# Clustered attention with a gated FFN behind it: transfers reordered over two queues, loads three pairs deep, RMS work in single steps

## The chip, the core and the metric

The kernel runs on one core of a Trainium2 chip. The core has five engines, each with its own in-order queue: TensorE (PE, its weight loads shown as PEld), VectorE (DVE), ScalarE (ACT), GpSimd (POOL) and SyncE (SP). SP does no arithmetic here, it issues DMA transfers; ACT and POOL issue some as well. The metric is the device time of one execution in microseconds, lower is better.

## What is computed

```python
# q, k, v: (4, 8, 768, 64) f32; centroids: (8, 16, 64) f32
q_assign = argmax(einsum('bhsd,hcd->bhsc', q_n, c_n), -1)   # q_n, k_n, c_n: rows scaled to norm 1
k_assign = argmax(einsum('bhsd,hcd->bhsc', k_n, c_n), -1)
mask = q_assign[:, :, :, None] == k_assign[:, :, None, :]
scores = where(mask, q @ k.T / 8, -1e9)
attn_out = softmax(scores) @ v                              # (4, 8, 768, 64)
x = attn_out.transpose(0, 2, 1, 3).reshape(3072, 512)
xn = x / sqrt(mean(x * x, -1) + 1e-6) * rms_g
g = xn @ w_gate                                             # 512 x 1536
out = (g * sigmoid(g) * (xn @ w_val)) @ w_out               # 1536 x 512, out (3072, 512) f32
```

Queries attend only to keys whose nearest of 16 centroids is the same one.

## The kernel before

The 32 slots (4 batches of 8 heads) run in order, two heads making a pair, 16 pairs in all. The scores of a slot are 768 x 768, cut into 9 chunks of 512 columns. One chunk is one step of the main loop, so a slot has 9 steps, a pair 18, a batch 72, all of it 288 steps. A schedule written out by hand sets the order on every engine: `at(step, fn)` hangs a piece of work on a step, and each engine does its instructions in the order in which the program emits them.

A step holds: the chunk's score matmuls (`score_chunk`, L241) and the exp of them on ACT (L244), one piece of the FFN if one is due (`ffn_next`), one group of the PV matmuls of the slot before (`pv_group`, L255, in steps 2 to 7 of a slot), at step 8 of a slot the division by the row sums on DVE (`pv_norm`, L264 and L265), and then what hangs on the step.

What hangs on steps, by pair: `load_pair` brings q, k and v of a pair from HBM (five transfers, 3 x 384 KB). The eight parts of `prep_parts` prepare a pair two pairs ahead of its use: three groups of four transposes on TensorE (`t_group`, L172, with a copy out of PSUM on DVE or ACT, L175 and L177), the bf16 casts on POOL (L182), the routing matmuls against the centroids (`assign`, sp, L195), two parts of argmax on DVE that end in ohT (L202 to L215), and the cast of v (L186). The second argmax part issues eight small transfers that put the one-hot rows under the operands (`aug<-ohT`, L220). These added rows make the score matmul itself subtract the mask. The parts of pair `pi` hang on steps 0, 2, 4, 5, 8, 9, 11 and 9 behind `18 * (pi - 2)`; pairs 0 and 1 are prepared ahead of the loop.

By batch: `rms_parts` has six sums of squares (ACT and DVE by turns, L279 and L282), the inverse root on POOL (`ir`, L287 and L288), then the scaled rows xn on DVE (L296), each followed by a transposing transfer into xnT, issued by SP (L298). These follow a batch's last pair, at steps 9 to 15 of the next batch. The FFN of a batch begins `LAG` steps into the next batch, one piece a step: a gate group gp, a value group vp (L318, four matmuls each), and, for the half batch before, an output group dp (L347). tanh of gp is on ACT (L323), the products uu and gvT on DVE (L327 and L333). The FFN of the last batch runs alone behind the loop. The FFN's first half batch reads three of the six xn transposes.

Weights come in twelve transfers from POOL's queue (`w_load`), which also turn them into bf16: four each of wg, wv and wo. PSUM holds two transpose buffers (`ps_t`, shared by t_group and assign), two for scores, two for gp and vp, one each for the PV sums and dp.

Of the kernel before, what the change touches and what calls it, by code (L numbers as in the profile page):

```python
# [9 lines left out]
BF16 = mybir.dt.bfloat16  # L10
AX = mybir.AxisListType.X
ALU = mybir.AluOpType
# [7 lines left out]
def kernel(  # L20
# [12 lines left out]
    nc = tc.nc  # L33
    B, H, S, D = q.shape
    NC = centroids.shape[1]
    DM, DF = moe_w_gate.shape
    P = 128
# [11 lines left out]
    out_v = out.rearrange("(b p t) d -> b p t d", b=B, t=ST)  # L49

    const = ctx.enter_context(tc.tile_pool(name="const", bufs=1))
    ld = ctx.enter_context(tc.tile_pool(name="ld", bufs=2))
    prep = ctx.enter_context(tc.tile_pool(name="prep", bufs=2))
    small = ctx.enter_context(tc.tile_pool(name="small", bufs=2))
    ptp = ctx.enter_context(tc.tile_pool(name="ptp", bufs=2))
# [10 lines left out]

    loads = {}

    def load_pair(pi, eng2=None):
        b, hp = divmod(pi, NP)  # L70
        tiles = []
        for src, nm, eng in ((q, "q_in", nc.sync), (k, "k_in", eng2 or nc.sync)):
            tl = ld.tile([P, ST, 2, D], F32, name=nm, tag=nm)
            for a in range(2):
                eng.dma_start(out=tl[:, :, a, :],
                              in_=src[b, 2 * hp + a].rearrange("(p t) d -> p t d", p=P))
            tiles.append(tl)
        tl = ld.tile([P, 2, ST * D], F32, name="v_in", tag="v_in")
        nc.sync.dma_start(
            out=tl, in_=v[b, 2 * hp:2 * hp + 2].rearrange("h (p t) d -> p h (t d)", p=P))  # L80
        tiles.append(tl)
        loads[pi] = tiles

    c_in = const.tile([P, D], F32, name="c_in")
    nc.scalar.dma_start(out=c_in, in_=centroids.rearrange("h c d -> (h c) d"))
    load_pair(0, nc.scalar)
    load_pair(1)
    g_b = const.tile([P, DM], F32, name="g_b")


# [68 lines left out]
    def prep_parts(pi):  # L159
        st = pi % NSET  # L160
        qk32 = [None]
        parts = []

        def t_group(g):
            if g == 0:
                qk32[0] = prep.tile([P, 2 * S], F32, name="qk32", tag="qk32")
            q_in, k_in, v_in = loads[pi]
            tp = ps_t.tile([P, 4, P], F32, name="tp", tag="t")
            for i in range(4):
                side, t = divmod(4 * g + i, ST)  # L170
                src = (q_in, k_in)[side]
                nc.tensor.transpose(tp[:, i, :], src[:, t, :, :].rearrange("p a d -> p (a d)"), ident_f)  # L172
            dst = qk32[0][:, g * 512:(g + 1) * 512]
            if g == 1 or pi < 5:
                nc.vector.tensor_copy(dst, tp[:, :, :].rearrange("p a b -> p (a b)"))  # L175
# [12 lines left out]

        state = {}

        def assign():
            hp = pi % NP
            sp = ps_t.tile([P, HS], F32, name="sp", tag="t")
            for j in range(4):
                nc.tensor.matmul(sp[32 * j:32 * j + 32, :], lhsT=cbd[:, hp, :],  # L195
                                 rhs=qk32[0][:, j * HS:(j + 1) * HS], start=True, stop=True,
                                 tile_position=(0, 32 * j))
            state["sp"] = sp

        def argmax1():  # L200
            tr = prep.tile([P, HS], F32, name="tr", tag="tr")
            nc.vector.transpose(tr, state["sp"])  # L202
            mx = small.tile([P, HS // NC], F32, name="mx", tag="mx")
            trv = tr[:, :].rearrange("p (n c) -> p n c", c=NC)
            nc.vector.tensor_reduce(mx, trv, axis=AX, op=ALU.max)
            state["tr"], state["mx"] = trv, mx

        def argmax2():
            oh = prep.tile([P, HS], BF16, name="oh", tag="oh")
# [5 lines left out]
            nc.vector.transpose(ohT, oh)  # L215
            for a in range(2):
                for j in range(4):
                    side, half = divmod(j, 2)
                    eng = nc.scalar if pi == 0 and a else nc.sync
                    eng.dma_start(  # L220
                        out=aug[st][a][O0[a]:O0[a] + NC, side, half * HS:(half + 1) * HS],
                        in_=ohT[32 * j + NC * a:32 * j + NC * a + NC, :])
# [48 lines left out]
    def rms_parts(b):  # L271
        st = {}

        def sumsq(t):
            if t == 0:
                st["ss"] = small.tile([P, ST], F32, name="ss", tag="ss")
                st["jk"] = xp.tile([P, 2, DM], BF16, name="jk", tag="jk")
            if t % 2 == 0:
                nc.scalar.activation(st["jk"][:, 0, :], x_t[b][:, t, :], ACT.Square,  # L279
                                     accum_out=st["ss"][:, t:t + 1])  # L280
            else:
                nc.vector.scalar_tensor_tensor(st["jk"][:, 1, :], x_t[b][:, t, :], 1.0, x_t[b][:, t, :],  # L282
                                               op0=ALU.mult, op1=ALU.mult, accum_out=st["ss"][:, t:t + 1])

        def inv():
            ir = small.tile([P, ST], F32, name="ir", tag="ir")
            nc.gpsimd.tensor_scalar(ir, st["ss"], scalar1=1.0 / DM, scalar2=eps, op0=ALU.mult, op1=ALU.add)  # L287
            nc.gpsimd.tensor_tensor(ir, ir, mhalf, op=ALU.pow)  # L288
            st["ir"] = ir

        def norm(m):
            if m == 0:
                xnT[b] = xp.tile([P, DC, S], BF16, name="xnT", tag="xnT")
            for t in range(m * TH, (m + 1) * TH):
                xn = xp.tile([P, DM], BF16, name="xn", tag="xn", bufs=ST)
                nc.vector.scalar_tensor_tensor(xn, x_t[b][:, t, :], st["ir"][:, t:t + 1], g_b,  # L296
                                               op0=ALU.mult, op1=ALU.mult)
                nc.sync.dma_start_transpose(xnT[b][:, :, t * P:(t + 1) * P], xn)  # L298

        return [lambda t=t: sumsq(t) for t in range(ST)] + [inv, lambda: norm(0), lambda: norm(1)]  # L300


    gvT = {}
# [75 lines left out]
    def at(step, fn):  # L379
        extra.setdefault(step, []).append(fn)  # L380

    for i, part in enumerate(prep_parts(0)):
        part()
        if i == 1:
            put_centroids()
    for i, part in enumerate(prep_parts(1)):
        part()
    for a in range(2):
        nc.vector.memset(aug[2][a], 0.0)
    load_pair(2)  # L390
    load_pair(3)
    nc.sync.dma_start(out=g_b, in_=moe_rms_g.unsqueeze(0).to_broadcast([P, DM]))
    for pi in range(2, B * NP):
        base = 2 * NCH * (pi - 2)
        for fn, step in zip(prep_parts(pi), (0, 2, 4, 5, 8, 9, 11, 9)):
            at(base + step, fn)
        if pi + 2 < B * NP:
            at(base + 12, lambda pi=pi: load_pair(pi + 2))
    for i in range(12):
        at(3 + 6 * i, lambda i=i: w_load(i))  # L400
    for b in range(B):
        steps = (9, 9, 10, 10, 11, 11, 12, 13, 15)
# [59 lines left out]
```

## Time and profile before

| what | value |
|---|---|
| three runs | 401.71, 405.21 and 406.61 us; median 405.21 |
| the profiled execution | 406.12 us, its span 404.3 us |
| TensorE busy | 347.4 us (86% of the span) |
| ScalarE, VectorE, GpSimd busy | 229.8, 224.7 and 76.3 us |
| mean granted TensorE clock | 0.958 of full speed |
| DMA | 35.40 MB, mean 88 GB/s |

Rows of the profile are read so. A timeline row has start, length, engine, line, operation, output <- input, count, and in brackets how long the engine stood idle before and what released it. "SPq" is SP issuing a transfer, not the transfer itself. A row of the chain of waits has start, length and what it was. A row of busy time by stretch gives the stretch, its length, the busy time and the number of instructions of each engine, the granted clock of TensorE, the mean busy share of the 16 DMA engines and the GB/s. A row of a line's instructions gives the shortest, median and longest in ns. Rows of a DMA queue give packets, MB and the time of its packets as a share of 16 engines over the stretch.

### The profile page before, as it was taken

Reading aid. Unit: us, or ns where it says so; the run is one execution under the profiler, and the core shown is the slowest. Engines: PE = TensorE matmul, PEld = TensorE weight load, DVE = VectorE, ACT = ScalarE, POOL = GpSimd, SP = SyncE. Lnnn points to the kernel's source line nnn. Section 1 sums busy time; section 2 is a strip of 40 time slices with the busy share of each in tenths; the row PEclk is TensorE's granted clock in tenths of the full one; section 3 lists DMA queues with packets and bytes.
Section 4 is the critical chain, followed back from the end, with each engine's and each line's share of the span. In section 5 each row is a group of like instructions: output and inputs, shape, how many; then the busy total and the mean of one; then the engine's idle time right before and its main releaser. Section 6 shows DMA issues by size and latency. Waiting matters only on the chain.

```text
span 404.3 us, 7577 instructions
## 1 busy us (share of the span) xinstructions
PE 347.4 (86%) x2880; PEld 209.6 (52%) x2913; DVE 224.7 (56%) x443; ACT 229.8 (57%) x441; POOL 76.3 (19%) x80
## 2 busy tenths in 40 slices
PE   2706996884699999979999999989999996999996
PEld 1304664553456656546565656555666653555542
DVE  5542664347155665694647564876545577655540
ACT  1004997696367877666676767756777741222231
POOL 1531455531202030312021212303000001000000
PEclk9955999899689999999999999999999999999999
DMA  9129799973804042319150605041100004110011
GB/s 192 54 53 244 140 214 191 201 127 97 184 12 123 16 116 53 101 38 182 47 147 7 170 14 147 6 96 42 35 29 28 2 26 92 40 53 26 26 54 78
DMA packets 78212, 35.40 MB, mean 88 GB/s; under 512 B 66272, under 2 KB 73952, under 8 KB 78176
## 3 DMA queue, kind: packets, MB, share of 16 engines
q1 hardware_dynamic: 73584, 29.72, 29.8%
q0 software_dynamic: 2752, 4.72, 6.9%
q10 hardware_dynamic: 1840, 0.48, 0.6%
q8 instruction: 23, 0.38, 0.4%
q14 instruction: 13, 0.11, 0.1%
HBM read 28.61 MB, written 6.29 MB: 86 GB/s over the span
## 4 chain that ended last, share of the span: by engine, by line
PE 70%; DVE 9%; ACT 6%; DMA 6%; SPq 4%; issue 3%; POOL 1%; POOLq 0%; ACTq 0%; DVEq 0%
PE gp L318 14%; PE vp L318 14%; PE dp L347 13%; PE sc L241 13%; PE acc L255 7%; PE tp L172 5%; ACT pT L244 5%; PE sp L195 4%; DMA k_in<-in_k_dram 4%; DVE xn L296 3%; SPq L220 2%; DMA xnT<-xn 1%; DVE uu L327 1%; DVE jk L282 1%; DVE gvT L333 1%
## 5 line engine op out<-in xcount | busy, mean ns | idle before, releaser
L244 ACT ACTIVATE pT<-sc 128x512 bf16<-128x512 f32 x288 | 165.4, 597 | 96.4 <-PE sc L241 94.9
L241 PE MATMUL sc<-aug 128*128 128x512 bf16 (+1 forms) x384 | 111.3, 336 | 5.6 <-ACT pT L244 4.7
L327 DVE SCALAR_TENSOR_TENSOR uu<-th,gp 128x384 f32<-128x384 f32 x96 | 53.1, 553 | 81.7 <-ACT th L323 81.7
L318 PE MATMUL vp<-xnT,wv 128*128 128x384 bf16 x384 | 78.7, 328 | 6.6 <-DVE gvT L333 6.3
L318 PE MATMUL gp<-xnT,wg 128*128 128x384 bf16 x384 | 78.7, 328 | 5.9 <-DMA xnT<-xn 4.2
L255 PEld LDWEIGHTS <-pT 128*128 128x128 bf16 x1152 | 63.2, 100 | 38.2 <-DVE x L265 4.6
L182 POOL CAST aug<-qk 64x1536 bf16<-64x1536 f32 x32 | 46.8, 1464 | 178.1 <-ACT qk L177 98.5
L323 ACT ACTIVATE th<-gp 128x384 f32<-128x384 f32 x96 | 47.2, 492 | 56.5 <-PE gp L318 53.9
L347 PE MATMUL dp<-wo,gvT 128*128 128x512 bf16 x255 | 71.0, 379 | 4.9 <-DVE ob L355 2.2
L255 PE MATMUL acc<-vbf,pT 128*128 128x65 bf16 x1152 | 69.4, 196 | 4.2 <-DVE x L265 4.0
L333 DVE TENSOR_TENSOR gvT<-uu,vp 128x384 bf16<-128x384 f32 x96 | 52.7, 549 | 7.0 <-PE vp L318 1.6
L318 PEld LDWEIGHTS <-wg 128*128 128x128 bf16 x384 | 37.3, 98 | 35.7 <-issue 7.8
L318 PEld LDWEIGHTS <-wv 128*128 128x128 bf16 x384 | 37.4, 98 | 27.3 <-issue 9.0
L241 PEld LDWEIGHTS <-aug 128*128 128x128 bf16 x384 | 34.6, 100 | 20.5 <-issue 6.3
L347 PEld LDWEIGHTS <-gvT 128*128 128x128 bf16 x288 | 27.9, 97 | 29.5 <-issue 4.6
L175 DVE COPY qk<-tp 128x512 f32<-128x512 f32 x26 | 17.9, 690 | 39.4 <-PE tp L172 39.4
L172 PE MATMUL tp<-ident_f,q_in 128*128 128x128 f32 x96 | 18.2, 308 | 18.5 <-DMA q_in<-in_q_dram 18.5
L172 PE MATMUL tp<-ident_f,k_in 128*128 128x128 f32 x96 | 18.9, 313 | 7.3 <-DMA k_in<-in_k_dram 4.7
L172 PEld LDWEIGHTS tp<-ident_f,q_in 128*128 128x128 f32 x96 | 12.7, 157 | 22.9 <-issue 15.9
L296 DVE SCALAR_TENSOR_TENSOR xn<-x,ir,g_b 128x512 bf16<-128x512 bf16 x24 | 16.5, 746 | 4.2 <-POOL ir L288 4.2
L265 DVE TENSOR_TENSOR x<-acc,inv 128x384 bf16<-128x384 f32 x32 | 17.8, 557 | 1.1
L177 ACT COPY qk<-tp 128x512 f32<-128x512 f32 x22 | 12.9, 586 | 7.9 <-PE tp L172 7.9
(48 smaller groups left out, 155.8 us busy)
## 6 DMA issues: line engine op xcount, KB each, us to landing
q_in<-in_q_dram SPq DMA_DIRECT2D x32, 192.0 KB, 3.7
v_in<-in_v_dram SPq DMA_DIRECT2D x16, 384.0 KB, 4.6
out_dram<-ob SPq DMA_DIRECT2D x24, 256.0 KB, 2.0
k_in<-in_k_dram SPq DMA_DIRECT2D x30, 192.0 KB, 4.0
aug<-ohT SPq DMA_DIRECT2D x124, 12.0 KB, 1.8
wg<-in_moe_w_gate_dram POOLq DMA_DIRECT2D x4, 384.0 KB, 5.6
wv<-in_moe_w_val_dram POOLq DMA_DIRECT2D x4, 384.0 KB, 7.7
wo<-in_moe_w_out_dram POOLq DMA_DIRECT2D x4, 384.0 KB, 8.8
```

What stands on the lines that cost most here:

```text
L172: nc.tensor.transpose(tp[:, i, :], src[:, t, :, :].rearrange("p a d -> p (a d)"), ident_f)
L175: nc.vector.tensor_copy(dst, tp[:, :, :].rearrange("p a b -> p (a b)"))
L182: nc.gpsimd.tensor_copy(aug[st][a][r, :, :].rearrange("p s n -> p (s n)"), qk32[0][r, :])
L241: nc.tensor.matmul(sc[:, o:o + n], lhsT=ag[:, 1, kc * P:(kc + 1) * P], rhs=ag[:, 0, qo:qo + n], start=True, stop=True)
L244: nc.scalar.activation(pts[slot][:, j * CH:(j + 1) * CH], sc, ACT.Exp, scale=scale)
L255: nc.tensor.matmul(acc[:, g, :], lhsT=pts[slot][:, kc * S + g * P:kc * S + (g + 1) * P], rhs=vb[:, a, kc, :], start=(kc == 0), stop=(kc == ...
L296: nc.vector.scalar_tensor_tensor(xn, x_t[b][:, t, :], st["ir"][:, t:t + 1], g_b, op0=ALU.mult, op1=ALU.mult)
L318: nc.tensor.matmul(pt[:, :HS], lhsT=w[:, dc, fc * P:(fc + 1) * P], rhs=xnT[b][:, dc, m * HS:(m + 1) * HS], start=(dc == 0), stop=(dc == DC ...
L323: nc.scalar.activation(th, pt[:, :HS], ACT.Tanh, scale=0.5)
L327: nc.vector.scalar_tensor_tensor(uu, th, 1.0, pt[:, :HS], op0=ALU.add, op1=ALU.mult)
L333: nc.vector.tensor_tensor(gvT[half][:, fc, :], uu, pt[:, :HS], op=ALU.mult)
L347: nc.tensor.matmul(dp, lhsT=gvT[hf][:, f, tl * P:(tl + 1) * P], rhs=wo[:, f, :], start=(f == 0), stop=(f == FC - 1))
```

## The change

- The load pool has three buffers of each tensor instead of two.
- The first two pairs' loads: before, SP issued nine and ACT the two of pair 0's k. Now SP issues the two of pair 0's q, and ACT all others.
- Pair 2's load and g_b (the RMS gains) are issued ahead of pair 1's preparation, pair 3's at step 3, pair 4's at step 17, and pair `pi + 2` of the others at step 6 of pair `pi`'s 18 instead of 12.
- Pair 2's own preparation stands six steps later, at steps 6 to 17.
- Weight loads: eight at steps 4, 14, ... 74 and four at 84, 96, 108 and 120, instead of twelve at steps 3, 9, ... 69.
- The copies out of the transpose buffers: pair 0's second one goes to ACT, pair 5's first and third to DVE.
- RMS: one part per step. `norm` does one of six xn and its transposing transfer instead of three; the 13 parts stand at steps 9 to 25 of a batch instead of 9 parts at 9 to 15. xn has three buffers instead of six.
- `LAG` is 26 instead of 24.

```diff
-    ld = ctx.enter_context(tc.tile_pool(name="ld", bufs=2))
+    ld = ctx.enter_context(tc.tile_pool(name="ld", bufs=3))
...
-    load_pair(0, nc.scalar)
-    load_pair(1)
+    load_pair(0, (nc.sync, nc.scalar, nc.scalar))
+    load_pair(1, (nc.scalar, nc.scalar, nc.scalar))
...
-            if g == 1 or pi < 5:
+            if (g == 1) != (pi == 0) or 0 < pi < 6:
                 nc.vector.tensor_copy(dst, tp[:, :, :].rearrange("p a b -> p (a b)"))
...
-        def norm(m):
-            if m == 0:
+        def norm(t):
+            if t == 0:
                 xnT[b] = xp.tile([P, DC, S], BF16, name="xnT", tag="xnT")
-            for t in range(m * TH, (m + 1) * TH):
-                xn = xp.tile([P, DM], BF16, name="xn", tag="xn", bufs=ST)
...
+            xn = xp.tile([P, DM], BF16, name="xn", tag="xn", bufs=3)
...
+    load_pair(2)
+    nc.sync.dma_start(out=g_b, in_=moe_rms_g.unsqueeze(0).to_broadcast([P, DM]))
     for i, part in enumerate(prep_parts(1)):
         part()
...
-    load_pair(2)
-    load_pair(3)
-    nc.sync.dma_start(out=g_b, in_=moe_rms_g.unsqueeze(0).to_broadcast([P, DM]))
...
+        steps = (0, 2, 4, 5, 8, 9, 11, 9) if pi > 2 else (6, 8, 10, 11, 14, 15, 17, 15)
...
-            at(base + 12, lambda pi=pi: load_pair(pi + 2))
+            at(base + 6 if pi > 2 else 17, lambda pi=pi: load_pair(pi + 2))
+    at(3, lambda: load_pair(3))
...
-    LAG = 24
+    LAG = 26
```

How the instructions stand on the engines, before and now. First SP's queue at the program's start, as it was before; the number behind q_in and its like is the buffer of one pair's load, that behind ohT belongs to one pair's routing:

```order
L75 DMA q_in_95<-in_q_dram 128x6x64 x2
L79 DMA v_in_101<-in_v_dram 128x2x384
L75 DMA q_in_103<-in_q_dram 128x6x64 x2
L75 DMA k_in_106<-in_k_dram 128x6x64 x2
L79 DMA v_in_109<-in_v_dram 128x2x384
L220 DMA aug00_125<-ohT_196 16x384 x4
L220 DMA aug10_131<-ohT_240 16x384 x4
L220 DMA aug11_133<-ohT_240 16x384 x4
L75 DMA q_in_253<-in_q_dram 128x6x64 x2
```

The last row is pair 2's load; it stood behind the rows of pair 0 (ohT_196) and pair 1 (ohT_240). The same place of SP's queue now, on to pair 3's load:

```order
L76 DMA q_in_95<-in_q_dram 128x6x64 x2
L221 DMA aug00_125<-ohT_196 16x384 x4
L76 DMA q_in_207<-in_q_dram 128x6x64 x2
L76 DMA k_in_210<-in_k_dram 128x6x64 x2
L80 DMA v_in_213<-in_v_dram 128x2x384
L388 DMA g_b_111<-in_moe_rms_g_dram 128x512
L221 DMA aug10_131<-ohT_249 16x384 x4
L221 DMA aug11_133<-ohT_249 16x384 x4
L76 DMA q_in_276<-in_q_dram 128x6x64 x2
```

Pair 2's load (q_in_207 and the next two) and g_b stand between pair 0's rows and pair 1's, and pair 3's load (q_in_276) behind pair 1's rows. Next SP's queue around the first batch's transposes of xn, before:

```order
L220 DMA aug00_125<-ohT_1148 16x384 x4
L220 DMA aug01_127<-ohT_1148 16x384 x4
L75 DMA q_in_1169<-in_q_dram 128x6x64 x2
L75 DMA k_in_1172<-in_k_dram 128x6x64 x2
L79 DMA v_in_1175<-in_v_dram 128x2x384
L298 DMA_TRANSPOSE xnT_1190<-xn_1191 128x4x128
L298 DMA_TRANSPOSE xnT_1190<-xn_1194 128x4x128
L298 DMA_TRANSPOSE xnT_1190<-xn_1197 128x4x128
```

These are pair 6's rows, pair 8's load and the first three transposes. The same place now:

```order
L76 DMA q_in_1091<-in_q_dram 128x6x64 x2
L76 DMA k_in_1094<-in_k_dram 128x6x64 x2
L80 DMA v_in_1097<-in_v_dram 128x2x384
L221 DMA aug00_125<-ohT_1150 16x384 x4
L221 DMA aug01_127<-ohT_1150 16x384 x4
L298 DMA_TRANSPOSE xnT_1222<-xn_1223 128x4x128
L298 DMA_TRANSPOSE xnT_1222<-xn_1237 128x4x128
L298 DMA_TRANSPOSE xnT_1222<-xn_1244 128x4x128
```

Pair 8's load went from between the rows and the transposes to ahead of the rows. Last DVE's queue at the same place in the program, before (jk are the squares, xn the scaled rows, inv and x the two instructions of `pv_norm`):

```order
L282 SCALAR_TENSOR_TENSOR jk,ss<-x 128x512 x2
L210 TENSOR_TENSOR oh<-tr,mx 128x384
L212 TENSOR_SCALAR oh<-oh 64x384
L215 STREAM_TRANSPOSE ohT<-oh 128x384
L282 SCALAR_TENSOR_TENSOR jk,ss<-x 128x512
L296 SCALAR_TENSOR_TENSOR xn<-x,ir,g_b 128x512 x6
L264 RECIPROCAL inv<-acc 128x6
L265 TENSOR_TENSOR x<-acc,inv 128x6x64
L175 COPY qk_1248<-tp 128x512
```

And now:

```order
L283 SCALAR_TENSOR_TENSOR jk,ss<-x 128x512
L211 TENSOR_TENSOR oh<-tr,mx 128x384
L213 TENSOR_SCALAR oh<-oh 64x384
L216 STREAM_TRANSPOSE ohT<-oh 128x384
L283 SCALAR_TENSOR_TENSOR jk,ss<-x 128x512 x2
L265 RECIPROCAL inv<-acc 128x6
L266 TENSOR_TENSOR x<-acc,inv 128x6x64
L296 SCALAR_TENSOR_TENSOR xn<-x,ir,g_b 128x512 x3
L176 COPY qk_1230<-tp 128x512
L296 SCALAR_TENSOR_TENSOR xn<-x,ir,g_b 128x512 x3
L265 RECIPROCAL inv<-acc 128x6
```

One square went behind ohT, the six xn behind `pv_norm`, and pair 7's copy between the third and the fourth.

More of the change, by code (lines that the diff above doesn't have):

```diff
@@ L67, with load_pair @@
     loads = {}
-    def load_pair(pi, eng2=None):
+    def load_pair(pi, engs=None):
         b, hp = divmod(pi, NP)
+        engs = engs or (nc.sync, nc.sync, nc.sync)
         tiles = []
-        for src, nm, eng in ((q, "q_in", nc.sync), (k, "k_in", eng2 or nc.sync)):
+        for src, nm, eng in ((q, "q_in", engs[0]), (k, "k_in", engs[1])):
             tl = ld.tile([P, ST, 2, D], F32, name=nm, tag=nm)
@@ L78, in load_pair @@
         tl = ld.tile([P, 2, ST * D], F32, name="v_in", tag="v_in")
-        nc.sync.dma_start(
+        engs[2].dma_start(
             out=tl, in_=v[b, 2 * hp:2 * hp + 2].rearrange("h (p t) d -> p h (t d)", p=P))
@@ L289, in inv @@
             st["ir"] = ir
-        def norm(m):
-            if m == 0:
+        def norm(t):
+            if t == 0:
                 xnT[b] = xp.tile([P, DC, S], BF16, name="xnT", tag="xnT")
-            for t in range(m * TH, (m + 1) * TH):
-                xn = xp.tile([P, DM], BF16, name="xn", tag="xn", bufs=ST)
[L296 to L300, printed above, removed]
+            xn = xp.tile([P, DM], BF16, name="xn", tag="xn", bufs=3)
+            nc.vector.scalar_tensor_tensor(xn, x_t[b][:, t, :], st["ir"][:, t:t + 1], g_b,
+                                           op0=ALU.mult, op1=ALU.mult)
+            nc.sync.dma_start_transpose(xnT[b][:, :, t * P:(t + 1) * P], xn)
+        return ([lambda t=t: sumsq(t) for t in range(ST)] + [inv]
+                + [lambda t=t: norm(t) for t in range(ST)])
     gvT = {}
@@ L389 @@
         nc.vector.memset(aug[2][a], 0.0)
-    load_pair(2)
-    load_pair(3)
-    nc.sync.dma_start(out=g_b, in_=moe_rms_g.unsqueeze(0).to_broadcast([P, DM]))
     for pi in range(2, B * NP):
         base = 2 * NCH * (pi - 2)
-        for fn, step in zip(prep_parts(pi), (0, 2, 4, 5, 8, 9, 11, 9)):
+        steps = (0, 2, 4, 5, 8, 9, 11, 9) if pi > 2 else (6, 8, 10, 11, 14, 15, 17, 15)
+        for fn, step in zip(prep_parts(pi), steps):
             at(base + step, fn)
         if pi + 2 < B * NP:
-            at(base + 12, lambda pi=pi: load_pair(pi + 2))
-    for i in range(12):
-        at(3 + 6 * i, lambda i=i: w_load(i))
+            at(base + 6 if pi > 2 else 17, lambda pi=pi: load_pair(pi + 2))
+    at(3, lambda: load_pair(3))
+    for i in range(8):
+        at(4 + 10 * i, lambda i=i: w_load(i))
+    for i in range(4):
+        at(84 + 12 * i, lambda i=i: w_load(8 + i))
     for b in range(B):
-        steps = (9, 9, 10, 10, 11, 11, 12, 13, 15)
+        steps = (9, 10, 11, 12, 13, 14, 15, 17, 18, 19, 21, 23, 25)
         for fn, step in zip(rms_parts(b), steps):
             at(H * NCH * (b + 1) + step, fn)
-    LAG = 24
+    LAG = 26
     def extras(step):
```

## The prediction

> **What bounds the kernel now.** I first asked in which stretches TensorE does nothing, with the table of busy time by stretch.
>
> ```profile
> core 0: us, PE busy (x) PEld busy (x) DVE busy (x) ACT busy (x) POOL busy (x), PEclk, DMA share, GB/s
> 24.00:33.00 9.00, 0.00 (x0) 0.00 (x0) 1.10 (x2) 0.00 (x0) 0.00 (x0) 0.50 0.63 126
> 39.60:50.20 10.60, 9.89 (x121) 6.58 (x121) 6.05 (x11) 9.75 (x19) 5.09 (x7) 1.00 0.79 153
> 60.80:76.70 15.90, 11.46 (x121) 7.47 (x121) 5.31 (x11) 10.85 (x21) 7.10 (x8) 0.89 0.92 179
> 87.80:112.50 24.70, 14.88 (x129) 9.25 (x130) 11.61 (x24) 13.05 (x28) 7.16 (x8) 0.83 0.59 132
> 148.10:168.50 20.40, 20.21 (x184) 12.54 (x187) 11.50 (x25) 14.19 (x27) 4.36 (x5) 1.00 0.30 76
> 168.50:192.80 24.30, 20.74 (x184) 12.51 (x186) 17.63 (x38) 15.53 (x33) 5.72 (x6) 1.00 0.46 92
> 253.90:277.40 23.50, 20.62 (x183) 12.54 (x190) 17.66 (x37) 15.54 (x32) 5.31 (x6) 1.00 0.25 61
> 328.00:341.00 13.00, 9.13 (x58) 4.79 (x58) 11.15 (x23) 3.90 (x10) 1.52 (x2) 1.00 0.20 50
> ```
>
> Rows two to seven are each one pair (18 steps). A pair of attention alone takes 10.6 us, with ACT at 9.75. A pair with all of the FFN beside it takes 20.4, and there TensorE is full: nothing but its work counts. What exceeds these prices is waiting. TensorE's own timeline names it:
>
> ```profile
> 33.16 1.08 PE L172 MATMUL tp<-ident_f,q_in 128*128 128x128 f32 x4 [12.35 <-DMA q_in<-in_q_dram]
> 72.00 0.41 PE L172 MATMUL tp<-ident_f,k_in 128*128 128x128 f32 x2 [3.81 <-DMA k_in<-in_k_dram]
> 100.47 0.51 PE L255 MATMUL acc<-vbf,pT 128*128 128x65 bf16 x6 [4.02 <-DVE x L265]
> 108.30 1.44 PE L318 MATMUL gp<-xnT,wg 128*128 128x384 bf16 x4 [3.52 <-DMA xnT<-xn]
> ```
>
> Who made these late stands in SP's timeline. SP issues one transfer after another: loads, the mask rows (aug<-ohT) and the transposes of xn.
>
> ```profile
> 16.72 11.83 SPq L220 DMA_DIRECT2D aug<-ohT  x12
> 28.65 1.29 SPq L75 DMA_DIRECT2D q_in<-in_q_dram  x2
> 31.42 0.93 SPq L79 DMA_DIRECT2D v_in<-in_v_dram  x1
> 60.93 1.44 SPq L75 DMA_DIRECT2D q_in<-in_q_dram  x2
> 65.51 9.24 SPq L220 DMA_DIRECT2D aug<-ohT  x8
> 74.86 1.30 SPq L75 DMA_DIRECT2D q_in<-in_q_dram  x2
> 93.17 5.98 SPq L220 DMA_DIRECT2D aug<-ohT  x8
> 99.25 1.29 SPq L75 DMA_DIRECT2D q_in<-in_q_dram  x2
> 103.01 7.86 SPq L298 DMA_TRANSPOSE xnT<-xn  x6
> ```
>
> Pair 2's load stands behind both pairs' mask rows until 28.65. The third batch of rows (9.24 us for eight, where six is usual) went into full rings. The first transposes stand behind a load from 99.25 to 103.0. The chain of waits gives the milestones (sp x8 is the routing of a pair, step 8 of its 18):
>
> ```profile
> 17.99 2.30 PE sp L195 x8
> 23.01 0.59 DVE ohT L215
> 40.77 4.28 ACT pT L244 x8
> 87.81 0.78 PE sp L195 x8
> 91.74 0.61 ACT jk L279 x2
> ```
>
> **The start, part by part.** ACT's queue now issues nine loads before ACT's table load, and the second copy of pair 0 moves from DVE to ACT. SP issued nearly the same series before:
>
> ```profile
> 4.15 4.19 SPq L75 DMA_DIRECT2D k_in<-in_k_dram  x2
> 8.39 0.82 SPq L79 DMA_DIRECT2D v_in<-in_v_dram  x1
> 2.56 1.28 ACT L100 ACT_TABLE_LOAD   x1 [2.56 <-issue]
> 9.23 0.69 DVE L175 COPY qk<-tp 128x512 f32<-128x512 f32 x1 [1.27 <-PE tp L172]
> 1.87 6.53 DMA k_in<-in_k_dram
> ```
>
> Pair 1's k was held for 4.19 us, and the last issue ended at 9.2. If ACT is held alike, the table load ends at 10.5 and the copy at about 11.3, against 9.9. TensorE's next transposes need that PSUM buffer, so everything is 1.4 us later, a little of it won back: I take +1.2. The bound on the other side: ACT isn't held, and k, behind no other load on its ring, lands up to 2 us before 8.40: -1.5. The Trainium skill (DMA: Bandwidth & Descriptors, "Issuing engines are not separate DMA queues") says that issuing from several engines saves issue time alone, since all share 16 engines; by that the -1.5 falls away and the sum stays.
>
> Step 0 was at 20.3 (end of pair 1's sp) and is then at 21.5. Pair 2's transposes stand at step 6 instead of 0, so six scores come first, at ACT's 4.28 / 8 = 0.535 us: step 6 at 24.7. On SP, pair 0's four mask rows run from 17.9 at 0.62 each (the last eight of the twelve before ran from ohT's end, 23.60, to 28.55) to 20.4; pair 2's load follows. A load lands in:
>
> ```profile
> q_in<-in_q_dram SPq DMA_DIRECT2D x32, 192.0 KB, 3.7
> ```
>
> Its second q half is issued at 21.1 and lands at 24.8. The 12.35 us wait is gone, to within some tenths.
>
> What is late next: pair 3's load. It needs no buffer any more (three deep), but on SP it stands behind pair 2's load (28.65 to 32.35, 3.8 with the gap: ends 24.2), g_b (one more issue, 0.6) and pair 1's eight rows. These, now queued behind the load, wait until 24.8 for their ohT anyway (23.6 + 1.2) and end at 29.8: issued from 29.9, second q half 30.6, landed 34.3. Step 18 is at 21.5 + 18 x 0.56 = 31.6 (0.56 between 0.535 and 10.6 / 18 = 0.59). TensorE waits 2.7 us; between 0 (steps slower) and 6 (a weight load beside it).
>
> **Attention, steps 18 to 98.** Weights go from one in 6 steps to one in 10. The DMA queues of 45 to 73 us:
>
> ```profile
> q0 software_dynamic: 1470, 3.11, 61.3%
> q1 hardware_dynamic: 7437, 2.60, 39.3%
> ```
>
> q0 is the weights: 17.2 us of the 28 for 3.11 MB, 2.2 per 384 KB. q1 takes 4.2 us per MB, 5.0 for a pair's 1.18 MB (3 x 384 KB). Before, a pair of 10.6 us asked for 3 x 2.2 + 5.0 = 11.6, more than there is; now 1.8 x 2.2 + 5.0 = 9.0, 85%. So I let the 3.81 us wait go and the pace be 10.6 a pair. SP has about 3.8 + 8 x 0.62 = 8.8 us of issue per pair: also fits, and loads 4 to 8 come 4 us or more ahead by that count. Moving pair 5's copies to DVE is hidden (DVE 6 of 10.6). Pair 6's routing (step 80) is at 31.6 + 2.7 + 62 x 0.59 = 70.9, and with pair 6's copies on ACT at 71.3 (the pair from 76.7 to 87.8, which had them, took 11.1), against 87.81.
>
> From there it goes by SP. Its rows began 5.4 us behind sp and were out at 99.15, 11.3 behind it: 82.6 now. The load that followed has moved ahead. For the transposes:
>
> ```profile
> L298 SPq DMA_TRANSPOSE xnT<-xn x24: 1192/1217/2221, 103.0 to 342.6; - x24
> DMA to landing us min/median/max: 2.4/2.5/4.3
> ```
>
> The FFN's first half needs three: the third is issued at 82.6 + 2 x 1.3 = 85.2 and lands at 87.7. TensorE would be at step 98 at 71.3 + 11.1 + 3 x 0.61 (ACT's squares) = 84.2, and waits 3.6 us: **first FFN matmul at 87.8, against 108.3: 20.5 us**. The 4.02 us wait falls away inside this: it was for pv_norm, queued on DVE behind six xn in a row,
>
> ```profile
> 95.66 4.06 DVE L296 SCALAR_TENSOR_TENSOR xn<-x,ir,g_b 128x512 bf16<-128x512 bf16 x6 [1.96 <-POOL ir L288]
> ```
>
> which now come behind that pv_norm. The FFN starts two steps later in the program, so two more scores and PV groups are behind it already: at most 2 x 9.89 / 18 = 1.1 us of TensorE, of which transposes and routing have a part; I take 0.8: 21.3. xn has three buffers, so DVE's fourth waits for the first transpose to land; behind the sixth, which waits for the third transpose (87.7), stands the next pv_norm, 1.5 us on, before PV needs it at step 101.
>
> Clock: TensorE ran at about half after such waits.
>
> ```profile
> 108.00:115.00 7.00, 6.70 (x38) 3.08 (x39) 2.70 (x6) 2.27 (x4) 0.83 (x1) 0.56 0.28 56
> ```
>
> Since I leave a wait of 3.6 us at the same place, I let this stretch stand; without it some 7 x (1 - 0.56) = 3 us more are won. The Trainium skill (TensorE: Matmul & The Clock Gate, "Why this matters for your kernels") puts the limit at gaps of about 3 us: by it the sum has a step there: a second wait of 2.9 instead of 3.6 would give 377.5 - 0.7 - 3.0 = 373.8. The trace agrees as far as it goes (slow after 3.52); no gap of it near 3 us shows the limit.
>
> **RMS behind the FFN.** Three boundaries cost 24.3 - 20.4 = 3.9, 23.5 - 20.4 = 3.1 and 13.0 - 9.13 = 3.9: 10.9. There DVE does its three xn in a row while FFN results wait. One per step fits a 20.4 us pair (DVE 17.6), but DVE is in order and still stands for ir: I leave 1 us at the first two and 2.5 at the last, whose steps are short. Won: 6.4, between 0 and 10.9. The later wo loads (last at step 120, first use at 136) have 16 steps: nothing.
>
> **The sum.** 21.3 + 6.4 = 27.7; span 404.3 - 27.7 = 376.6. The profiled execution took 406.12 and its span is 1.8 less; the median of the runs is 405.21. 378.4 x 405.21 / 406.12 = **377.5**.
>
> **Rivals.** *Full cover*: ACT isn't held (2.7), half of the two waits (3.2) and half of the RMS rest (2.2) go as well, with some clock (1.5): 368. For it: the two waits are small differences between times counted from single rows, and vanish if SP is 0.1 us faster per issue. Against: SP's order makes them. Chance 0.20. *RMS in parts wins nothing*: DVE, waiting for ir or for a transpose with only three buffers, holds up the FFN at each boundary, and a row batch of 9 us doubles the wait at step 98: 377.5 + 6.4 + 3.6 = 387. DVE's share speaks against. 0.15. *The rings stay full*: the loads don't come early because SP is held in issuing, as from 60.93 to 74.86: 13.9 a pair, 4.5 for a load and 9.3 for eight rows. Six loads and five batches from 29.9: 103.4, the FFN at 108.5, and only the 7.2 of the other terms are won: 398. Against: 85% instead of 109% demand. 0.07. *Slower*: the clock in the FFN stage. That stage is 289 us of full TensorE. The row
>
> ```profile
> 109.00:130.00 21.00, 20.46 (x186) 12.70 (x184) 11.16 (x23) 14.32 (x28) 2.46 (x3) 0.88 0.30 73
> ```
>
> shows 0.88 over 21 us of it. Should the denser work be granted 0.88 throughout, 289 / 0.88 adds 39 us: 417. It eats the whole gain below 0.91. Against: 1.00 from 148.1 to 168.5 with TensorE 99% busy. 0.03. The forecast has 0.55.
>
> **Numbers.** A measurement of this kernel tells about 2% from no change, that is 397 to 413. The range takes the forecast with its bounds, most of full cover and the RMS rival: 365 to 392. Faster by over 2%: 0.55 + 0.20 + 0.15 and a little of the third rival, 0.91; same 0.06; slower 0.03.
>
> **What would show it.** No wait of over 1 us for pair 2's q; one of 1 to 5 us for pair 3's q near 32; DMA share under 0.95 from 45 to 73 and pairs of 10.6; first gp at 85 to 91, behind xnT; pairs over an RMS boundary at 21 to 22 us. The forecast is wrong if ACT's first copy comes after 13 us, if eight rows still take 9 us on SP more than once, or if first gp comes after 95.

## The result, and the profile after

The changed kernel takes 386.32 us (median of 4 runs, 384.61 to 389.47) against 405.91 of before (4 runs, 401.71 to 406.98): 19.6 us less; the ratio on record is 0.955, 95% interval 0.947 to 0.963. In the later runs the executions of the kernel before fall into two groups, 399 to 404 us and a slower state of 405 to 412 that their ratios leave out; three of the four here and the profiled one (406.12) lie in the range of the second, so the gains against them are probably some us too large, and fast against fast the changed kernel, run again, is at 0.964 (0.957 to 0.972). The forecast was 377.5 with 365 to 392 around it: the time lies inside, 9 us on the slow side of the forecast. The profiled execution of the changed kernel took 389.47 us, span 387.7, so by the two profiles the gain is 16.6 us against the 27.7 of the sum.

TensorE's timeline of the changed kernel, its long waits of the first 110 us (in brackets the idle time before, and its releaser):

```profile
33.87 0.63 PE L173 MATMUL tp<-ident_f,q_in 128*128 128x128 f32 x4 [1.55 <-DMA q_in<-in_q_dram]
39.06 0.66 PE L173 MATMUL tp<-ident_f,k_in 128*128 128x128 f32 x2 [3.69 <-DMA k_in<-in_k_dram]
102.32 1.44 PE L319 MATMUL gp<-xnT,wg 128*128 128x384 bf16 x4 [12.88 <-DMA xnT<-xn]
```

The waits of 12.35 us (pair 2's q), 3.81 (pair 5's k) and 4.02 (pv_norm behind six xn) are gone. In their place stand 5.2 us for pair 3's load, and one of 12.9 us where the FFN starts: it was 3.5. The first FFN matmul comes at 102.3 instead of 108.3; that is later than the 95 us which the prediction gave as a sign that it is wrong. The chain of waits gives the routing of pairs 2, 3, 4, 5 and 6, and what the FFN waited for:

```profile
29.66 0.78 PE sp L196 x8
44.38 0.78 PE sp L196 x8
55.00 0.78 PE sp L196 x8
65.62 0.78 PE sp L196 x8
76.71 0.78 PE sp L196 x8
...
93.57 1.35 SPq L298
...
95.03 1.28 SPq L298
...
96.40 5.83 DMA xnT<-xn
```

Attention runs at 10.6 us a pair from 44.4 on, as counted. But pair 6's rows, whose routing was at 76.7, were on SP only from 87.7. SP's timeline of the changed kernel:

```profile
40.64 1.29 SPq L76 DMA_DIRECT2D q_in<-in_q_dram  x2
...
44.47 1.23 SPq L76 DMA_DIRECT2D q_in<-in_q_dram  x2
45.79 2.13 SPq L76 DMA_DIRECT2D k_in<-in_k_dram  x2
48.01 3.05 SPq L80 DMA_DIRECT2D v_in<-in_v_dram  x1
51.16 6.45 SPq L221 DMA_DIRECT2D aug<-ohT  x8
57.70 1.30 SPq L76 DMA_DIRECT2D q_in<-in_q_dram  x2
59.10 3.61 SPq L76 DMA_DIRECT2D k_in<-in_k_dram  x2
62.80 2.56 SPq L80 DMA_DIRECT2D v_in<-in_v_dram  x1
65.50 5.71 SPq L221 DMA_DIRECT2D aug<-ohT  x8
...
83.01 1.30 SPq L76 DMA_DIRECT2D q_in<-in_q_dram  x2
...
87.72 5.75 SPq L221 DMA_DIRECT2D aug<-ohT  x8
93.57 4.38 SPq L298 DMA_TRANSPOSE xnT<-xn  x3
```

From 40.6 to the transposes SP has no pause. A load that issues in 3.8 us when free takes 6.6 (from 44.47) and 7.7 (from 57.70). Four pairs, from 44.47 to 93.47, take SP 12.2 us each, where TensorE and ACT need 10.6. SP, which does no arithmetic, sets the pace of the stage.

Behind the start of the FFN it is the other way round; the table by stretch, of the changed kernel (a plain pair, one over the first RMS boundary, the last boundary):

```profile
140.10:160.50 20.40, 20.40 (x186) 12.71 (x184) 11.85 (x24) 14.38 (x28) 3.76 (x3) 1.00 0.30 76
160.50:181.20 20.70, 20.70 (x186) 12.81 (x185) 17.83 (x37) 15.83 (x33) 5.63 (x5) 1.00 0.38 85
304.00:330.00 26.00, 22.23 (x150) 12.11 (x149) 19.55 (x39) 7.45 (x17) 1.52 (x2) 1.00 0.21 51
```

Over the boundary TensorE has no idle time left. At the last one it still stands for 26.0 - 22.2 = 3.8 us.

### The profile page after: what moved, and what is told of

Read it like the earlier page. It is cut to its first block, busy times and chain, and to the rows that moved or that the text cites. A ratio compares the mean times of both kernels' runs of the same rounds, so it can differ in the third digit from the quotient of the medians.

```text
span 387.7 us, 7630 instructions
## 1 busy us (share of the span) xinstructions
PE 344.9 (89%) x2913; PEld 208.2 (54%) x2913; DVE 227.6 (59%) x444; ACT 229.0 (59%) x440; POOL 76.2 (20%) x80
## 4 chain that ended last, share of the span: by engine, by line
PE 80%; ACT 7%; DMA 6%; DVE 3%; SPq 2%; issue 1%; POOLq 0%; POOL 0%; ACTq 0%; DVEq 0%
PE sc L242 16%; PE gp L319 16%; PE dp L348 15%; PE vp L319 15%; PE acc L256 8%; PE tp L173 6%; ACT pT L245 6%; PE sp L196 4%; DMA xnT<-xn 3%; DMA k_in<-in_k_dram 2%; SPq L221 1%; DMA q_in<-in_q_dram 1%; SPq L298 1%; DVE xn L296 1%; ACT jk L280 0%
## 5 line engine op out<-in xcount | busy, mean ns | idle before, releaser
L319 PE MATMUL gp<-xnT,wg 128*128 128x384 bf16 x384 | 78.9, 328 | 15.0 <-DMA xnT<-xn 12.9
L319 PE MATMUL vp<-xnT,wv 128*128 128x384 bf16 x384 | 78.7, 328 | 1.2 <-DVE gvT L334 1.2
L348 PE MATMUL dp<-wo,gvT 128*128 128x512 bf16 x288 | 76.0, 379 | 1.6 <-ACT ob L354 1.1
L256 PE MATMUL acc<-vbf,pT 128*128 128x65 bf16 x1152 | 68.6, 195 | 0.0
L319 PEld LDWEIGHTS <-wg 128*128 128x128 bf16 x384 | 37.5, 98 | 45.6 <-issue 17.4
L319 PEld LDWEIGHTS <-wv 128*128 128x128 bf16 x384 | 37.5, 98 | 26.9 <-issue 2.5
L242 PEld LDWEIGHTS <-aug 128*128 128x128 bf16 x384 | 34.7, 99 | 22.5 <-issue 10.6
L296 DVE SCALAR_TENSOR_TENSOR xn<-x,ir,g_b 128x512 bf16<-128x512 bf16 x24 | 18.9, 812 | 17.2 <-DMA xnT<-xn 16.3
L196 PE MATMUL sp<-qk,cbd 128*32 128x384 f32 x128 | 16.5, 564 | 0.8 <-DVE qk L176 0.8
```

Of the source, the lines that this page charges most:

```text
L242: nc.tensor.matmul(sc[:, o:o + n], lhsT=ag[:, 1, kc * P:(kc + 1) * P], rhs=ag[:, 0, qo:qo + n], start=True, stop=True)
L256: nc.tensor.matmul(acc[:, g, :], lhsT=pts[slot][:, kc * S + g * P:kc * S + (g + 1) * P], rhs=vb[:, a, kc, :], start=(kc == 0), stop=(kc == ...
L319: nc.tensor.matmul(pt[:, :HS], lhsT=w[:, dc, fc * P:(fc + 1) * P], rhs=xnT[b][:, dc, m * HS:(m + 1) * HS], start=(dc == 0), stop=(dc == DC ...
L348: nc.tensor.matmul(dp, lhsT=gvT[hf][:, f, tl * P:(tl + 1) * P], rhs=wo[:, f, :], start=(f == 0), stop=(f == FC - 1))
```

## The experiments

The ideas to be told apart: that weight packets hold SP up (W), that SP simply has too many transfers (S), that the earliest late load costs the time (pair 3's), and how much the change's own parts are worth. "First gp" is the first FFN matmul in each run's own profile. The kernel before, run beside the others on each chip, had medians of 402.6 to 408.4 us.

### No weights on the way

```diff
-            nc.gpsimd.dma_start(out=(wg, wv)[kind][:, j, :], ...)
+            nc.vector.memset((wg, wv)[kind][:, j, :], 0.01)
...
-            nc.gpsimd.dma_start(out=wo[:, 3 * j:3 * j + 3, :], ...)
+            nc.vector.memset(wo[:, 3 * j:3 * j + 3, :], 0.01)
```

> The weights are not loaded: where a weight load stood, DVE fills that part of the weight tile with a constant, so the FFN computes with constants in place of the real weights, at the same size and count of matmuls. Theory W (weight packets fill the rings and hold SP in issuing the loads): a pair's load is issued in 3.3 to 4 us everywhere (6.6, 7.7 and 6.5 us in the changed kernel for pairs 5, 6 and 7), pair 6's mask rows start as soon as their ohT is ready, the third xn transpose lands in 2.5 us instead of 5.8, the first FFN matmul comes at 86 to 91 us instead of 102.3, and the time is 371 to 376 us. Theory S (SP has too many transfers to issue in this stage, whatever else travels): loads still take 6 to 8 us to issue, only the landing gets shorter, first FFN matmul at 98 to 99, time 382 to 384 us.

Measured: 374.08 us (373.46 to 374.72), ratio 0.934 [0.931, 0.938]. SP's and TensorE's timelines of this run (L218, L295 and L316 are the L221, L298 and L319 of the others):

```profile
53.19 1.30 SPq L76 DMA_DIRECT2D q_in<-in_q_dram  x2
54.58 1.91 SPq L76 DMA_DIRECT2D k_in<-in_k_dram  x2
56.59 0.58 SPq L80 DMA_DIRECT2D v_in<-in_v_dram  x1
57.31 5.33 SPq L218 DMA_DIRECT2D aug<-ohT  x8
...
76.06 5.38 SPq L218 DMA_DIRECT2D aug<-ohT  x8
81.53 7.10 SPq L295 DMA_TRANSPOSE xnT<-xn  x5
```

```profile
86.73 0.82 PE L316 MATMUL gp<-xnT,wg 128*128 128x384 bf16 x4 [2.57 <-DMA xnT<-xn]
```

Pair 6's load, 7.7 us to issue with weights beside it, takes 4.0 (53.19 to 57.17), pairs 7's and 8's 3.4 and 3.7; only pair 5's, issued straight behind pair 4's, still takes 5.3. The third transpose lands 2.4 us after its issue. TensorE's waits for pair 3's q and k shrink from 1.55 and 3.69 us to 0.85 and 0.47. So it is the weight loads that hold SP up: W holds, but for pair 5's load. First gp at 86.7 and pair 6's routing at 71.4 are also close to what the forecast had for the real kernel (87.8 and 71.3). The count of the stage fits a kernel whose weights cost SP nothing, though errors in it cancel: the start came 1.7 us earlier than counted (19.8 against 21.5) and the waits for pair 3 were 1.3 us instead of 2.7, but the first 18 steps took 12.4 us instead of 10.1. That a full queue of transfers is what stops SP is the likely reading, though no view shows a queue's filling.

### Wo out of the transposes' way

```diff
-        at(84 + 12 * i, lambda i=i: w_load(8 + i))
+        at(114 + 4 * i, lambda i=i: w_load(8 + i))
```

> The last four weight loads (wo) move from steps 84, 96, 108 and 120 to 114, 118, 122 and 126, so on POOL's queue they stand behind pair 8's casts instead of beside the first transposes of xn. Theory W: the third transpose lands in 2.5 us instead of 5.8, pair 8's load is issued a little faster, first FFN matmul at 97 to 99 us, time 381 to 383 us; no wait for wo at step 136. Theory S: the landing was slow for the transposes' own sake or behind loads, first FFN matmul stays at 101 to 103 and the time at 385 to 388 us.

Measured: 382.88 us (382.11 to 383.37). The chain of waits and TensorE's timeline:

```profile
94.06 2.42 DMA xnT<-xn
```

```profile
96.58 1.44 PE L319 MATMUL gp<-xnT,wg 128*128 128x384 bf16 x4 [8.08 <-DMA xnT<-xn]
```

The landing is back at 2.4 us, and the FFN starts 5.7 us earlier. The landing makes 3.4 of that, which is also what the median gained; the other 2.3 come from SP, whose rows ended at 91.3 instead of 93.5. POOL's timeline of the changed kernel tells why the loads of steps 96 and 108 were there at all:

```profile
91.00 0.86 POOL L155 DMA_DIRECT2D wo<-in_moe_w_out_dram  x1
91.91 0.82 POOL L187 CAST vbf<-v_in 128x768 bf16<-128x768 f32 x1
92.68 0.79 POOL L155 DMA_DIRECT2D wo<-in_moe_w_out_dram  x1
```

A step is a place in the order, not a time. POOL waits only for the casts' inputs, so between two pairs' casts it issues every weight load it finds: two at once, both before step 98, at the transposes' own moment.

### Pair 8's load behind the transposes

```diff
-            at(base + 6 if pi > 2 else 17, lambda pi=pi: load_pair(pi + 2))
+            at({2: 17, 6: 98, 7: 104}.get(pi, base + 6), lambda pi=pi: load_pair(pi + 2))
```

> Pair 8's load moves from step 78 to 98 and pair 9's from 96 to 104, so on SP they stand behind the first batch's transposes instead of ahead of pair 6's mask rows. If SP's queue sets the start of the FFN (it issued without a pause from 40.6 to 93.5 us in the changed kernel), pair 6's rows start at 83 instead of 87.7, the first FFN matmul comes 4 to 5 us earlier, at 97 to 98, and the time is 381 to 383 us. If the transposes' landing beside the weights sets it, 0 to 2 us are won. If pair 8's load then comes late for step 108, TensorE waits there for q by up to 4 us and nothing is won.

Measured: 382.05 us (379.63 to 385.3); first gp at 98.2. SP's timeline:

```profile
77.91 10.76 SPq L221 DMA_DIRECT2D aug<-ohT  x16
88.76 11.34 SPq L298 DMA_TRANSPOSE xnT<-xn  x6
```

Pairs 5's and 6's rows stand together and end at 88.7 instead of 93.5; the transposes still land slowly (7.5 us at the most), since wo is beside them. The rows end 4.8 us earlier, and the FFN starts 4.1 us earlier, as the third transpose took 6.6 us to land instead of 5.8. So what SP does ahead of the transposes moves the FFN's start nearly one for one, and the load taken from there is not missed: no wait of 1 us or more follows up to 118 us.

### Pair 3's load first

```diff
     load_pair(2)
+    load_pair(3)
...
-    at(3, lambda: load_pair(3))
```

> Pair 3's load is issued directly behind pair 2's, ahead of pair 1's mask rows, instead of behind them. TensorE's waits for pair 3's q and k (1.6 and 3.7 us in the changed kernel, and half clock behind them) should go, or a wait of about 1 us for pair 1's rows take their place. If TensorE's own path sets the start of the FFN, pair 3's routing comes at 38 to 40 us instead of 44.4, the first FFN matmul at 96 to 98 and the time is 380 to 382 us. If SP's queue sets it, the rows of pair 2 still wait for their ohT until about 34 us, load 4 is issued at about 40 us as now, and everything SP does from there stands as it stood: the earlier routing is given back, first FFN matmul at 100 to 103, time 384 to 388 us.

Measured: 387.01 us (385.09 to 390.65), the same as the changed kernel. TensorE and SP:

```profile
36.42 0.58 PE L242 MATMUL sc<-aug 128*128 128x512 bf16 x1 [6.04 <-DMA aug<-ohT]
100.22 1.44 PE L319 MATMUL gp<-xnT,wg 128*128 128x384 bf16 x4 [11.50 <-DMA xnT<-xn]
```

```profile
40.33 1.29 SPq L76 DMA_DIRECT2D q_in<-in_q_dram  x2
```

The wait for pair 3 turned into one of 6 us for pair 1's rows, which now stand behind two loads. And SP is at pair 4's load at 40.3, as in the changed kernel at 40.6. From there on it does what it did, as S and W both say. So the waits at 30 to 40 us are real, but not what the time hangs on.

### All three, and two of them

The run of all three has the three diffs above.

> The edits of the three runs before together: wo behind pair 8's casts, pairs 8 and 9 loaded behind the transposes, pair 3 loaded ahead of pair 1's rows. If SP's queue held up by weight packets sets the start of the FFN, the two gains on SP's queue add (5.7 for wo, 4.1 for the loads, less where TensorE comes next): rows of pair 6 from 81 us, third transpose landed at 92, first FFN matmul at 91 to 94 us, time 374 to 378 us. If they are one and the same gain, first FFN matmul at 96 and time 381 to 383 us.

Measured: 380.50 us (379.9 to 381.45), first gp at 95.0 with 4.6 us of waiting before it: 2.5 us above the range for gains that add. TensorE lost 7.1 us at step 18 to pair 1's rows. SP was late too: it had no pause from 31.4 to 97.5 us, came to pair 4's load at 43.3 (40.3 with pair 3's load first alone), and its rows for pairs 5 and 6 were out at 89.6, with the transposes straight behind them. So pair 3's load went back to its place behind pair 1's rows, and the other two edits stayed.

> Wo behind pair 8's casts and pairs 8 and 9 loaded behind the transposes, with pair 3's load left behind pair 1's rows. In the run with all three edits TensorE had lost 7.1 us at step 18, waiting for pair 1's rows, and stood at step 98 only 4.6 us before the transposes. If SP's queue sets the start, pair 6's rows start at 81 to 82 us, the third transpose lands near 92.5 and the first FFN matmul comes at 92 to 94 us: 377 to 380 us. If what pair 3's load costs TensorE counts by now, it is no better than all three, 380 to 382 us.

Measured: 378.36 us (377.7 to 378.89), ratio to before 0.944 [0.939, 0.948]. SP's rows for pairs 5 and 6 were out at 87.3, 2.3 us earlier than in the run of all three, and first gp is earlier by the same 2.3 us. So the third edit seems to have cost its time there through SP. First gp:

```profile
92.72 1.44 PE L319 MATMUL gp<-xnT,wg 128*128 128x384 bf16 x4 [4.30 <-DMA xnT<-xn]
```

The changed kernel was run beside it.

> The changed kernel as it is, beside the next two on the same chip, so that they can be set against it directly: 384 to 389 us, first FFN matmul at 100 to 103 us behind xnT.

It took 386.51 us (385.05 to 388.51), first gp at 100.8. The profile differs from the first one of the same kernel: first gp is 1.5 us earlier, and one wait of 5.5 us for pair 3's q stands in place of the two of 1.55 and 3.69. So a difference of 1.5 us in first gp between two runs can be chance. The version with two edits is 8.1 us faster than the changed kernel on the same chip, with no overlap of their executions; of the runs that load the weights it has the lowest median, though the next one is within 0.6 us of it.

### Part of the loads on another queue, and later weights

```diff
+            engs = (nc.sync, nc.sync, nc.gpsimd) if pi < 6 else None
...
-        at(4 + 10 * i, lambda i=i: w_load(i))
+        at(16 + 9 * i, lambda i=i: w_load(i))
```

> As the run before, and in addition the v loads of pairs 3 to 7 go on POOL's queue instead of SP's, and the eight loads of wg and wv start at step 16 instead of 4 (every 9 steps). If full rings on SP's queue are what holds it, SP has 12 transfers a pair instead of 13 and its ring less in it, holds of over 3 us for a load become rare, pair 3's q and k come without weight packets beside them (waits below 2 us), first FFN matmul at 87 to 90 us, time 373 to 377 us. If it is the shared DMA engines as such, whatever queue feeds them, SP is held as long on the transfers left and the first FFN matmul stays at 92 to 95 us, 377 to 381 us.

Measured: 378.96 us (378.22 to 380.22), no better; first gp at 93.0. SP was freed: a pair's four remaining load transfers took 2.6 to 3.5 us. But pair 6's routing came at 77.1, later than the 75.7 of the run with two edits, its rows ended at 87.7, and the FFN waited 3.2 us. TensorE had been late from step 18 on, with waits of 1.9 and 4.5 us at pair 3's transposes. Neither reading of the expectation fits wholly: SP was freed, and the time stayed. The next run has only the second of these edits: the weights later, v left on SP.

> As the run with wo and the loads of pairs 8 and 9 behind, and the eight loads of wg and wv at steps 16, 25, ... 79 instead of 4, 14, ... 74. It asks whether TensorE's 5.6 us wait for pair 3's q comes from weight packets beside that load. If so, pair 3's q and k cost it under 2 us, pair 6's routing comes at 71 to 73 us instead of 75.7; SP then decides, as its holds from 45 us on have the same weights beside them: first FFN matmul at 90 to 93 us, 376 to 379 us. If the wait is the load's place behind pair 1's rows alone, it stays at 4 to 6 us and the time at 378 to 379.5 us.

Measured, on another chip: 380.11 us (379.19 to 381.05), first gp at 93.6, waits for pair 3 of 2.5 and 2.8 us. The run does not answer its question. The first weight load, now at step 16, was issued at 31.05, behind pair 2's casts, again beside pair 3's k, which landed in 6.8 us. What the load costs with no weights beside it, only the run without weights shows: waits of 0.85 and 0.47 us. V on POOL's queue with the weights at their earlier steps was not run, so what that edit alone is worth stays open.

### The parts of the change

The three runs of this section were made on one chip. The changed kernel was not run beside them; its medians are 386.32 and 386.51 us.

```diff
-    for i in range(8):
-        at(4 + 10 * i, lambda i=i: w_load(i))
-    for i in range(4):
-        at(84 + 12 * i, lambda i=i: w_load(8 + i))
+    for i in range(12):
+        at(3 + 6 * i, lambda i=i: w_load(i))
```

> The changed kernel with the weight loads where they were (twelve at steps 3, 9, ... 69); all else stays. If the spreading is what frees the attention stage (the prediction: 109% of the DMA time asked for against 85%), SP is held longer between 45 and 75 us, TensorE waits for loads there again, and the time is 390 to 396 us. If the spreading gives back in front of the FFN what it wins before (two of the late loads run beside the first transposes), the third transpose lands in 2.5 us again, first FFN matmul stays at 99 to 105 and the time at 383 to 389 us.

Measured: 386.43 us (385.86 to 388.96): the spreading as such is worth nothing here. SP's timeline shows what the earlier weights cost:

```profile
51.02 10.72 SPq L221 DMA_DIRECT2D aug<-ohT  x8
61.85 2.54 SPq L76 DMA_DIRECT2D q_in<-in_q_dram  x2
64.48 5.99 SPq L76 DMA_DIRECT2D k_in<-in_k_dram  x2
```

The holds are longer, TensorE waits 5.7 us for rows at 79, but the third transpose, with no weights beside it, then lands in 2.4 instead of 5.8: first gp at 102.6, as in the changed kernel.

The RMS work as it was:

```diff
-        def norm(t):
+        def norm(m):
...
-        steps = (9, 10, 11, 12, 13, 14, 15, 17, 18, 19, 21, 23, 25)
+        steps = (9, 9, 10, 10, 11, 11, 12, 13, 15)
...
-    LAG = 26
+    LAG = 24
```

> The changed kernel with the RMS work as it was (three xn at a time, nine parts at steps 9 to 15, six xn buffers, LAG 24). If the RMS parts are worth what the pairs over a boundary show (24.3 and 23.5 us before, 20.1 now), these two pairs take 23 to 24 us again, the first FFN matmul stays near 102 us but is two steps earlier in the program (0.8), and the time is 393 to 396 us. If the gain there came from loads that no longer stand on SP's queue beside the transposes, the pairs stay at 20 to 21 and the time is 386 to 389 us.

Measured: 393.11 us (390.93 to 395.22), 6.7 slower than the changed kernel's two medians and 6.4 to 6.7 slower than the other two runs of this section. Its boundary pairs:

```profile
153.40:176.90 23.50, 20.60 (x183) 12.52 (x190) 17.63 (x37) 15.53 (x32) 5.30 (x6) 1.00 0.27 65
237.90:261.40 23.50, 20.62 (x184) 12.54 (x190) 17.66 (x37) 15.54 (x33) 5.31 (x6) 1.00 0.25 61
```

They are 3.4 us each above the 20.1 of the changed kernel. First gp came at 95.8, not near 102. Half of that is SP, whose rows ended at 90.5 instead of 93.5; the other half is the landing: the first three transposes, four to six steps earlier in the order, landed (the third in 2.4 us) before POOL issued the two wo loads at 96.0 and 98.8. One part per step seems to cost something at the FFN's start, and it wins more behind it.

The first loads and pair 0's second copy as they were:

```diff
-    load_pair(0, (nc.sync, nc.scalar, nc.scalar))
-    load_pair(1, (nc.scalar, nc.scalar, nc.scalar))
+    load_pair(0, (nc.sync, nc.scalar, nc.sync))
+    load_pair(1)
...
-            if (g == 1) != (pi == 0) or 0 < pi < 6:
+            if g == 1 or pi < 6:
```

> The changed kernel with the first loads as they were (all but the two of pair 0's k on SP) and pair 0's second copy on DVE again. The prediction counted the split as a loss of 1.2 us (ACT held by its loads); the changed kernel's trace shows pair 1's routing ending at 20.0 instead of 20.3 us, a gain of 0.3. By that the time is 386 to 388 us, and pair 1's routing ends at 20.2 to 20.5 us; by the prediction's count it ends at about 19 and the time is 384 to 386 us.

Measured: 386.70 us (385.54 to 387.08), pair 1's routing ending at 20.34: the split over two queues moves the start by 0.3 us and the time not at all.

## Why the prediction was right, and where its sum was off

The direction, and the waits that go, were right: pair 2's load, pair 5's k, pv_norm behind xn. That the time lies inside the range is partly luck. The first FFN matmul came 14.5 us later than forecast, and 377.5 + 14.5 is 392.0, the end of the range; what brought it back is that more was won behind that matmul than counted, and that the median lies 3.1 us below the profiled execution. What was off are sizes, and they can be put to the steps of the sum.

**The start**: taken at +1.2, measured at -0.3. ACT was held much as pictured, but the step behind it was wrong. The timeline of the changed kernel:

```profile
4.62 3.38 ACTq L76 DMA_DIRECT2D k_in<-in_k_dram  x2
9.25 1.09 PE L173 MATMUL tp<-ident_f,k_in 128*128 128x128 f32 x4 [0.64 <-DVE cbd L142]
10.23 0.57 ACT L178 COPY qk<-tp 128x512 f32<-128x512 f32 x1
```

"TensorE's next transposes need that PSUM buffer" does not hold: they ran at 9.25, ahead of ACT's copy, released by DVE's copy out of the centroids' transpose. So they took the buffer of the centroids' transpose, not the one that ACT copied from. Only the routing waits for ACT's copy, and k came early enough to make up for it.

**Pair 3's load**: taken at 2.7 us of waiting for q and none for k. Measured 1.55 and 3.69, and half clock behind the second. k landed 6.95 us after its issue, not 3.7 to 4.0: a weight load was issued on POOL at 31.38, beside it; without weights it landed in 3.6. Pair 6's routing came at 76.7 instead of 71.3, and the 5.4 us are these: the start -1.5, the first 18 steps +2.2 (12.3 us instead of 10.1), the two waits +2.5, the steps behind them +2.2 (39.2 us instead of 37.0, with the clock at half from 39 to beyond 42).

**The step that failed**: "SP has about 3.8 + 8 x 0.62 = 8.8 us of issue per pair: also fits, and loads 4 to 8 come 4 us or more ahead by that count". Its 0.62 us for a transfer is the price of an SP that nothing holds. With weight packets beside it SP took 12.2 us a pair; in the run without weights it took 9.2 to 9.5 for each of the three from 53.2 to 81.4 us. The rival of full rings, with 13.9 and a chance of 0.07, had the place right: SP's holds did go on, though milder. Pair 6's rows began at 87.7 instead of 5.4 us behind their routing, at 82.1: 5.6 us. The argument from 85% DMA demand averages over a pair; POOL issues the weights two at a time (at 46 and 47, 57 and 58, and two at 69 us), and each two fall on a pair's load or just ahead of it.

**The transposes' landing**: taken at 2.5, measured 5.83, 3.3 us. The prediction looked at the moved wo loads for when they are needed (step 136), and not for when POOL would issue them.

These three make 14.3 of the 14.5 us by which the first FFN matmul came later than forecast (102.3 against 87.8).

**Behind the first FFN matmul**: RMS was taken at 6.4 of 10.9. From first gp to the end the kernel before took 296.0 us and the changed one 285.4; less the estimated 0.8 of the two steps, that is 9.8, 3.4 more than counted. Not all of it is RMS. The pairs over the first two of the three boundaries counted are free altogether (20.1 us from routing to routing, as in the pairs around them, where it was 24.3 and 23.5): 7.5 us, and the run with the RMS work as it was gives 6.7 of them back. The last boundary, where I expected to win 1.4, won nothing: 3.8 against 3.9. The rest is 3.8 us less between the first gp and the routing at 138.3 (before: 148.1), 0.2 us less for each other pair, and 1.5 us more at the end; what made the 3.8 was not looked into.

So 27.7 - 14.5 + 3.4 = 16.6 us, the difference of the two spans.

**The clock**: granted 1.00 or close to it throughout the FFN stage (0.99 as a mean over 102.3 to 387.7), so the slower rival's condition did not arise. The step that the prediction puts at gaps of 3 us is not that sharp in the traces, as the last section shows.

## What to carry to other kernels

A queue that only issues transfers is an engine like any other: count its time per stage with the price it pays when others load the same DMA engines, and look for the stretch where it never pauses. A step in a written order is no time on an engine that doesn't wait for that step's work; look at what an engine can run ahead to, and put a bulk transfer behind something that holds it. Taking a visible wait away early gains nothing while another queue sets the stage's end, as pair 3's load showed here.

## What the runs showed of the hardware

How long a gap TensorE may have before its clock halves is not one number in these traces. At the first gp, which waited for different times, four matmuls of 128x384 took 0.81 to 0.82 us behind gaps of 2.22 and 2.57 us, and 1.44 behind 3.17, 3.19, 4.25 and more. But the granted clock can also fall behind a shorter gap, after the work has begun again. In the run without weights it was 1.00 up to 88.2 us and 0.51 from there to 91.7, 1.5 us behind the end of the gap of 2.57; four matmuls of the same size there took 0.82 and then 1.49 us:

```profile
86.73 0.82 PE L316 MATMUL gp<-xnT,wg 128*128 128x384 bf16 x4 [2.57 <-DMA xnT<-xn]
88.67 1.49 PE L316 MATMUL vp<-xnT,wv 128*128 128x384 bf16 x4
```

In the run with the weights later it fell to 0.50 at about 34.25 us, 0.7 us behind the gap of 2.52. In the changed kernel it fell at 36.4, only 1.0 us into the wait for pair 3's k, which had a gap of 1.55 us shortly before it. The run with v on POOL shows the other case, the clock already down when the work begins:

```profile
93.03 1.44 PE L319 MATMUL gp<-xnT,wg 128*128 128x384 bf16 x4 [3.17 <-DMA xnT<-xn]
```

The Trainium skill (TensorE: Matmul & The Clock Gate, "Why this matters for your kernels") advises no gaps over about 3 us. In two of these runs the clock was lost behind gaps of 2.5 and 2.6 us.

I had not expected a transfer from SBUF to SBUF, as the transposes are, to be slowed from 2.4 to 5.8 us by two 384 KB weight loads from another queue. The Trainium skill (DMA: Bandwidth & Descriptors, "Issuing engines are not separate DMA queues") says that transfers of all issuing engines interleave on the same 16 DMA engines; these runs agree. The same section of the Trainium skill calls the issue time saved by several queues usually small beside the transfer. Here the runs differ: on SP the issuing itself, at 12.2 us a pair with weight loads beside it, was the bound.
